# Block-sparse attention and a GELU feed-forward: the first batch as three units of eight query blocks instead of two of twelve

## The chip, the cores and the metric

The kernel runs on one core of a Trainium2 chip. A core has five engines that run in parallel and meet only through semaphores: TensorE (PE in the profile; its weight loads are listed apart as PEld), VectorE (DVE), ScalarE (ACT), GpSimd (POOL) and SyncE (SP, which only issues DMAs here). Each engine takes its instructions in the order in which the program emits them. The metric is the device time of one launch in microseconds; before the change it is 292.93 us, the median of three runs (292.79 to 292.94).

## What is computed

Attention over 4 batches, 8 heads, 768 positions and 64 dimensions, with a block mask of 32 by 32, and behind it a feed-forward layer over the 3072 tokens:

```python
scores = scale * np.matmul(q, k.transpose(0, 1, 3, 2))
mask = np.abs(blk_i - blk_j) <= window          # window = 1
mask = mask | (blk_i == 0) | (blk_j == 0) | (blk_i == n_blocks - 1) | (blk_j == n_blocks - 1)
for qb in range(n_blocks):
    for kb in sampled_blocks[qb]:               # three drawn blocks for each query block
        mask[qb * block:(qb + 1) * block, kb * block:(kb + 1) * block] = True
scores = np.where(mask, scores, -1000000000.0)
...
attn = attn / (np.sum(attn, axis=-1, keepdims=True) + 1e-09)
...
x = np.ascontiguousarray(attn_out.transpose(0, 2, 1, 3)).reshape(B * S, H * D)
h = x @ w_in                                    # 512 x 2048
g = 0.5 * h * (1.0 + erf(h * inv_sqrt2))
return (g @ w_out).astype(np.float32)           # 2048 x 512
```

Query blocks 0 and 23 see all 24 key blocks (they are called dense here). Each of the 22 others sees blocks 0 and 23, itself and its two neighbours, and the three drawn for it; a drawn block that is one of these, or a repeat, is replaced by a spare block whose values are zero.

## The kernel before

**Units.** The work is cut into units (class `Unit`, line 287). A unit is half a batch: twelve query blocks, as three quads of four. Each batch has a first unit with quads 1, 2 and 0 and the two dense blocks (`dense=True`, block 23 too), and a second with quads 3, 4 and 5. So there are eight units. The order of a unit is attention, then FFN1 (x times w_in and Gelu, `ffn1_step`, eight steps of eight matmuls with 384 columns), then FFN2 (g times w_out, 16 matmuls for each quad, `ffn2_pieces`). FFN2 of one unit is not run by itself: its matmuls are the filler of the next unit's attention, a number of them in each round, by a list written by hand (`quota`, and `tail` behind the last round). The first unit has no FFN2 to fill with; it gets products whose result nobody reads (`idle_products`).

**Attention.** `attention` (line 547) runs rounds. A sparse round is two query blocks over all heads: scores (TensorE, line 322, into a score tile of two banks of PSUM, pool `psA`, two buffers, which FFN1's `hp` tiles share), row maxima (VectorE, L347), exponentials (ScalarE, L364), transposition (VectorE, L381). A dense round is one dense block and half the heads (L350, L368, L386). When the rounds of a group are through (a quad, or the two dense blocks), `values` multiplies the probabilities with the values in two halves (TensorE, L442; its result `av` is in pool `psV`, one buffer), `divided` divides by the sums (VectorE, L457 to L461), and `outputs` transposes on TensorE (L471) and copies into `xT`, the input of FFN1 (ScalarE, L479). `when` and the unit's `ends` say in which round each half of each group's product is emitted. The second units of batches 0 to 2 also run the first two dense rounds of the batch after them (`ahead`). Between exponentials and Gelu ScalarE loads another function table (`table`, L392).

**Gathered keys.** The sparse scores read keys from one buffer `gb`, which holds for each query block of the unit at hand its neighbours' keys and the blocks at both ends (`gather_fixed`, lines 265 to 274) and its three drawn blocks, keys and values (`gather`, line 283, one copy for each, at an offset that a register holds). `gb` is refilled for the next unit while FFN1 of the present unit runs: first the fixed part and eight blocks on VectorE, then the rest on GpSimd. `hold_loads` (line 157) is a copy of one element on GpSimd: whatever is behind it on GpSimd, DMA issues too, waits until that element is written. In the very first unit keys and values are gathered apart: the keys first (from `k0`, which lies in the memory of `qT1`), the values by `values_of` in hooks of the rounds, since they land later.

**Loads.** All big loads are issued by GpSimd and share one queue in the order of issue: batch 0's keys, queries and values, w_in in two quarters and a half, w_out in two halves, then for batch 1 the keys (`load_by_token`, line 111) and queries. Keys and queries of batches 1 to 3 are turned by a transposing DMA that SP issues (`turn_keys` line 118, into `ptd`, which later holds dense probabilities; `turn_queries` line 121, into `qT1` for odd batches). SP also issues the stores of the outputs (L502), in the same order as the program. From `ptd` VectorE places the keys, scaled, into `kv` (`place_keys`, line 125; `next_keys` is this and a spare block). For batch 1 that is a hook of the second unit's attention:

```python
attention(nxt, filler, [3, 11, 2, 5, 3, 8, 1, 7, 1], (5,), ahead=units[n + 2],
          hooks={} if n else {
              3: [lambda: next_keys(1)]})
```

The main loop (line 678) goes over the units: refill of `gb` for the next unit and loads within FFN1's first step, FFN1, then the next unit's attention with this unit's FFN2 as its filler.

## Time and profile before

| what | value |
|---|---|
| median of three runs | 292.93 us |
| the profiled execution | 293.46 us, of which its span on the core is 291.7 us |
| mean granted TensorE clock in it | 0.988 |
| PE busy | 262.8 us (90% of the span) |
| DVE busy | 209.4 us (72%) |
| ACT busy | 204.3 us (70%) |
| POOL busy | 118.2 us (41%) |
| DMA | 25.36 MB in 90068 packets, 87 GB/s over the span |
| shares of the chain that ended last | PE 53%, DMA 17%, ACT 15%, POOL 6%, DVE 4%, issue 3% |

A row of the timeline has the start in us from the start of the span, the duration, engine, line and operation, out<-in by the program's names, the shape, how many instructions are merged, and in brackets how long the engine sat idle before them and which instruction ended that. A matmul's duration includes its way through the array; matmuls in a row overlap, so their pace is read from many of them. A row of the chain of waits has start, duration and what. A row of busy time by stretch has for each engine its busy us and number of instructions (PE, PEld, DVE, ACT, POOL), then the granted clock of TensorE as a share of full speed, the busy share of the DMA engines (summed over overlapping transfers) and GB/s. A row of a group has the number of instructions, their busy time in us and the mean duration in ns, then the idle time before them.

### The profile page before, as it was taken

The page shows a single profiled execution, that of the slowest core. Times are in us where ns is not written, and L with a number is a line of the kernel's source. Part 1 is how long each engine was busy: PE and PEld are TensorE (multiplying, and loading weights), DVE is VectorE, ACT ScalarE, POOL GpSimd, SP SyncE. Part 2 cuts the span into 40 slices and gives each one's busy share as a digit, 9 for nine tenths or more (in the row PEclk, how much of TensorE's full clock was granted, in tenths as well). Part 3 has the DMA queues.
Part 4 walks back from the last instruction along what each step waited for, and adds up shares of the span by engine and source line. Part 5 has one row for each costly group of instructions (what it writes and reads, how often), then busy time and mean ns, then how long its engine had stood idle before and what let it go on. Part 6 is the DMA issues. An engine that isn't in the chain of part 4 may idle for free.

```text
span 291.7 us, 11274 instructions
## 1 busy us (share of the span) xinstructions
PE 262.8 (90%) x4803; PEld 142.2 (49%) x4803; DVE 209.4 (72%) x477; ACT 204.3 (70%) x374; POOL 118.2 (41%) x217
## 2 busy tenths in 40 slices
PE   1799899854999999979998999999999999999995
PEld 1624555322553555535553556445544555356644
DVE  7699786816898969588997967798939877781000
ACT  8779656942667975787758966796778766976621
POOL 8789974935696004940594006910040014000000
PEclk9999999995999999999999999999999999999999
DMA  6995599999999215991399118991100110011001
GB/s 105 166 108 98 97 193 190 154 153 199 78 155 171 73 40 121 91 78 44 27 162 175 42 38 146 91 58 38 40 0 31 50 37 1 20 58 39 1 36 73
DMA packets 90068, 25.36 MB, mean 87 GB/s; under 512 B 81697, under 2 KB 86562, under 8 KB 90018
## 3 DMA queue, kind: packets, MB, share of 16 engines
q0 software_dynamic: 67792, 13.64, 87.5%
q1 hardware_dynamic: 22226, 11.01, 16.1%
q8 instruction: 37, 0.61, 1.0%
q14 instruction: 13, 0.11, 0.2%
HBM read 27.26 MB, written 6.29 MB: 115 GB/s over the span
## 4 chain that ended last, share of the span: by engine, by line
PE 53%; DMA 17%; ACT 15%; POOL 6%; DVE 4%; issue 3%; POOLq 1%; ACTq 0%
PE hp L492 19%; PE op L514 16%; PE av L442 9%; DMA ptd<-kn 6%; ACT pp L364 6%; DMA w_out_sb<-in_moe_w_out_dram 5%; ACT L392 4%; DMA kv<-in_v_dram 3%; POOL gb L283 3%; PE sc L322 3%; DMA qn<-in_q_dram 3%; ACT g L495 2%; PE tx L471 2%; PE av L543 2%; PE op L543 2%
## 5 line engine op out<-in xcount | busy, mean ns | idle before, releaser
L364 ACT ACTIVATE pp<-sc,nm 128x256 bf16<-128x256 f32 x176 | 75.3, 544 | 16.2 <-DVE nm L347 15.9
L514 PE MATMUL op<-w_out_sb,g 128*128 128x512 bf16 x336 | 86.4, 381 | 0.2
L492 PE MATMUL hp<-xT,w_in_sb 128*128 128x384 bf16 x512 | 85.0, 326 | 0.8 <-ACT xT L479 0.4
L495 ACT ACTIVATE g<-hp 128x768 bf16<-128x768 f32 (+1 forms) x72 | 52.1, 738 | 31.4 <-PE hp L492 31.4
L492 PEld LDWEIGHTS <-w_in_sb 128*128 128x128 bf16 x512 | 50.0, 98 | 36.0 <-issue 3.1
L347 DVE TENSOR_REDUCE nm<-sc 128x4 f32<-128x1024 f32 (+1 forms) x48 | 52.9, 1108 | 6.9 <-PE sc L322 6.9
L283 POOL COPY gb<-kv 128x388 bf16 (+1 forms) x87 | 36.7, 475 | 26.1 <-DVE gb L274 24.1
L514 PEld LDWEIGHTS <-g 128*128 128x128 bf16 x336 | 28.5, 97 | 35.4 <-issue 11.4
L283 DVE COPY gb<-kv 128x388 bf16 x177 | 39.8, 302 | 0.4 <-DMA qn<-in_q_dram 0.3
L442 PEld LDWEIGHTS <-pT 64*32 64x32 bf16 (+1 forms) x2400 | 26.3, 92 | 23.6 <-DVE pT L381 14.4
L381 DVE STREAM_TRANSPOSE pT<-pp 128x512 f32<-128x512 f32 (+1 forms) x48 | 31.5, 656 | 4.9 <-ACT pp L364 4.6
L442 PE MATMUL av<-kv,pT 64*32 64x130 bf16 (+1 forms) x1344 | 28.2, 223 | 7.4 <-DVE pT L381 7.2
L322 PE MATMUL sc<-gb,qT 64*32 64x256 bf16 x704 | 19.2, 274 | 7.4 <-ACT pp L364 4.7
L479 ACT COPY xT<-tx 128x512 bf16<-128x512 bf16 (+1 forms) x32 | 13.6, 450 | 15.3 <-PE tx L471 15.3
L157 POOL COPY mark<-g 1x1 bf16<-1x1 bf16 x2 | 7.0, 3504 | 42.4 <-ACT g L495 42.4
L133 POOL DMA_DIRECT2D kv<-in_v_dram x32 | 22.6, 715 | 1.3 <-DMA qn<-in_q_dram 1.2
L322 PEld LDWEIGHTS <-qT 64*32 64x32 bf16 x832 | 11.7, 90 | 23.3 <-issue 17.0
L368 ACT ACTIVATE pp<-sc,nm 128x768 bf16<-128x768 f32 x16 | 17.1, 1103 | 6.8 <-DVE nm L350 6.8
L111 POOL DMA_DIRECT2D qn<-in_q_dram x18 | 19.1, 1068 | 6.7 <-DMA w_out_sb<-in_moe_w_out_dram 6.2
L350 DVE TENSOR_REDUCE nm<-sc 128x1 f32<-128x768 f32 x16 | 15.0, 944 | 7.0 <-PE sc L322 6.7
L442 PE MATMUL av<-gb,pT 64*32 64x130 bf16 x1056 | 19.8, 223 | 0.0
L392 ACT ACT_TABLE_LOAD x15 | 19.2, 1283 | 0.3
(73 smaller groups left out, 230.1 us busy)
## 6 DMA issues: line engine op xcount, KB each, us to landing
out_dram<-os SPq DMA_DIRECT2D x23, 256.0 KB, 2.3
kv<-in_v_dram POOLq DMA_DIRECT2D x32, 96.0 KB, 6.9
kn<-in_k_dram POOLq DMA_DIRECT2D x18, 128.0 KB, 5.8
qn<-in_q_dram POOLq DMA_DIRECT2D x18, 128.0 KB, 5.5
w_out_sb<-in_moe_w_out_dram POOLq DMA_DIRECT2D x2, 1024.0 KB, 12.8
w_in_sb<-in_moe_w_in_dram POOLq DMA_DIRECT2D x2, 512.0 KB, 9.9
w_in_sb<-in_moe_w_in_dram POOLq DMA_DIRECT2D x1, 1024.0 KB, 9.0
kn<-in_k_dram POOLq DMA_DIRECT2D x2, 384.0 KB, 5.3
```

The source lines that it names most:

```text
L111: nc.gpsimd.dma_start(out=rows[:, c], in_=src[b, :, P * c:P * c + P].rearrange("h p d -> p h d"))
L133: nc.gpsimd.dma_start(out=kvs[b % 2][32 * hh:32 * hh + 32, 0:NB, c0:c0 + D], in_=v[b, h].rearrange("(n p) d -> p n d", p=BL))
L283: (engine or nc.vector).tensor_copy(sampled(unit.place[j], r)[:, None, c0:c1], src[:, bass.ds(at[j][r], 1), :])
L322: nc.tensor.matmul(o, lhsT=qT[rows, j // 4, pr, BL * (j % 4):BL * (j % 4) + BL], rhs=rhs(rows, pr), start=True, stop=True)
L347: nc.vector.tensor_reduce(out=nm[:, 0:2 * n].rearrange("p (g j) -> p g j", g=2), in_=A4[:, :, 0:n, :], op=ALU.max, axis=AX.X, negate=True)
L364: nc.scalar.activation(at[:, x // n, x % n], A[:, a:a + 256].rearrange("p (e c k) -> p e c k", e=2, k=BL), AF.Exp, bias=nm[:, x:x + 1])
L381: nc.vector.transpose(pt.rearrange("p g c x -> p (g c) x")[:, :, 64 * s:64 * (s + n)].bitcast(F32), pp[:, 0:512 * n].bitcast(F32).rearrang ...
L392: nc.scalar.activation(junk, zero[0:1, 0:1], func)
L442: nc.tensor.matmul(av[32 * s:32 * (s + w), h, V2 * G:V2 * G + V2], lhsT=pv[rows, c % 4, BL * s:BL * (s + w), c // 4], rhs=src[rows], start ...
L492: nc.tensor.matmul(hp[:, i, 0:T], lhsT=w_in_sb[:, ki, (m + i) * P:(m + i + 1) * P], rhs=xTs[n % 2][:, ki, 0:T], start=(ki == 0), stop=(ki ...
L495: nc.scalar.activation(g[:, m + i[0]:m + i[1], 0:T], hp[:, i[0]:i[1], 0:T], AF.Gelu)
L514: nc.tensor.matmul(op, lhsT=g[:, m, t * P:(t + 1) * P], rhs=w_out_sb[:, m, :], start=(m == 0), stop=(m == KOUT - 1))
```

## The change

Batch 0 becomes three units of two quads each: (1, 0) with the dense blocks, (2, 3), and (4, 5). Batches 1 to 3 keep two units of three quads. So there are nine units, and FFN1 of the first three has 256 columns instead of 384. A unit may now begin at a later column of its `xT` (`first`), because the third unit shares a buffer with the first, whose dense rounds already write block 23's columns.

With it go:

- the first unit has eight rounds instead of ten, 27 idle products instead of 43, and other rounds for its products (`when`); the fixed keys of its second sparse group are copied on ScalarE;
- `early` in this unit: the division of the group before the last stands behind the last transposition instead of ahead of the last round's end;
- the product of the unit's last group goes into a score tile (`psA`) instead of the one buffer of `psV`;
- GpSimd's order: no key copies for a third group; `ones(1)` ahead of the first value gather; w_in's second half behind the first value gather; w_out and batch 1's keys behind the second; batch 1's queries only in FFN1 of the first unit, behind a `hold_loads` and the gather of blocks 10 and 11; batch 1's values in FFN1 of the second unit;
- the refill of `gb` for unit 1 is blocks 8, 9 and 12 to 15 on VectorE and 10, 11 on GpSimd, for unit 2 blocks 16 to 19 and 20 to 22 (`SHARES`);
- `next_keys(1)` moves to the second round of the third unit's attention, and the first two dense rounds of batch 1 to the end of that unit;
- new lists of filler for the attentions of units 1, 2 and 3.

```diff
     class Unit:
-        def __init__(self, b, quads, dense):
-            self.b, self.quads, self.dense = b, quads, dense
+        def __init__(self, b, quads, dense, first=0):
+
+            self.b, self.quads, self.dense, self.c0 = b, quads, dense, first
...
-    units = [Unit(b, quads, dense) for b in range(B)
-             for quads, dense in (((1, 2, 0), True), ((3, 4, 5), False))]
+    units = [Unit(0, (1, 0), True), Unit(0, (2, 3), False), Unit(0, (4, 5), False, P)]
+    units += [Unit(b, quads, dense) for b in range(1, B)
+              for quads, dense in (((1, 2, 0), True), ((3, 4, 5), False))]
...
         if half == 0:
-            st[grp, "av"] = psV.tile([P, 2, 512], F32, name="av", tag="V")
+
+            pool, tag = (psA, "A") if grp == units[0].ends[len(units[0].rounds) - 1] else (psV, "V")
+            st[grp, "av"] = pool.tile([P, 2, 512], F32, name="av", tag=tag)
...
-            if weighed and last:
+            if weighed and last and not early:
                 divide()
...
         turned(rounds[n - 1][1])
+        if early:
+            divide()
...
     load_w_in(1)
-    others |= block_numbers(grps[2], POOL)
-    gather(units[0], grps[2], others, 0, KC, nc.gpsimd)
     others |= block_numbers(grps[0], POOL)
+    ones(1)
...
             gather(units[0], grps[t], others, KC, BW, nc.gpsimd)
-            if t == 1:
+            if t == 0:
                 load_w_in(1, 2)
-            if t == 2:
+            else:
                 load_w_out(0, 2)
                 load_w_out(1, 2)
                 load_by_token(kn, k, 1)
-                load_by_token(qn, q, 1)
-                others.update(block_numbers(J1[8:], POOL))
+                others.update(block_numbers(J0[9:], POOL))
...
-    attention(units[0], idle_products(43), [0, 3, 0, 8, 3, 7, 3, 2, 3, 3, 4], (3, 0, 4),
-              when=(5, 6, 7, 7, 8, 9, 10, 11),
-              hooks={0: [lambda: fixed(1)], 1: [lambda: fixed(2, nc.scalar.copy, 0)],
-                     3: [lambda: fixed(2, nc.scalar.copy, 1)], 4: [values_of(0)],
-                     6: [values_of(1)], 8: [values_of(2)], 10: [more_numbers(J1[:6])]})
+    attention(units[0], idle_products(27), [0, 3, 1, 8, 3, 7, 1, 0, 0], (0, 0, 4), early=True,
+              when=(5, 5, 6, 6, 8, 9),
+              hooks={1: [lambda: fixed(1, nc.scalar.copy, 0)], 3: [lambda: fixed(1, nc.scalar.copy, 1)],
+                     4: [values_of(0)], 6: [values_of(1)], 8: [more_numbers(J1[:4])]})
...
+    SHARES = {0: (J0[7:9] + J1[:4], J0[9:]), 1: (J1[4:8], J1[8:])}
...
             if s == 0:
-                if n == 0:
-                    turn_keys()
-                    turn_queries(1)
-                    hold_loads(sampled(nxt.place[J1[7]], NR - 1)[0:1, BW - 1:BW])
-                    gather(nxt, J1[8:], others, engine=nc.gpsimd)
-                    ones(1)
-                    hold_loads(qT1[0:1, 0:1])
-                    load_values(1)
+                if n <= 1:
+                    hold_loads(sampled(nxt.place[mine[-1]], NR - 1)[0:1, BW - 1:BW])
+                    gather(nxt, theirs, others, engine=nc.gpsimd)
+                    if n == 0:
+                        load_by_token(qn, q, 1)
+                        turn_keys()
+                        turn_queries(1)
+                        others.update(block_numbers(J1[8:], POOL))
+                    else:
+                        hold_loads(qT1[0:1, 0:1])
+                        load_values(1)
...
+        elif n == 0:
+            attention(nxt, filler, [3, 5, 5, 6, 5], (1, 0, 5), hooks={0: [more_numbers(J1[4:8])]})
+        elif n == 1:
+            attention(nxt, filler, [3, 7, 2, 5, 2, 5, 1], (4,), ahead=units[3],
+                      hooks={0: [more_numbers(J0[:3])], 1: [lambda: next_keys(1)]})
+        elif n == 2:
+            attention(nxt, filler, [1, 5, 3, 2, 1, 3, 3, 5, 3], (1, 0, 4))
         elif fresh:
             attention(nxt, filler, [1, 7, 4, 3, 1, 5, 4, 7, 6], (2, 0, 6))
         elif b + 1 < B:
-            attention(nxt, filler, [3, 11, 2, 5, 3, 8, 1, 7, 1], (5,), ahead=units[n + 2],
-                      hooks={} if n else {
-                          3: [lambda: next_keys(1)]})
+            attention(nxt, filler, [3, 11, 2, 5, 3, 8, 1, 7, 1], (5,), ahead=units[n + 2])
```

18 lines of the change are left out of this document (8 added, 10 removed).

## The prediction, made before the changed kernel was run

> **What bounds the kernel now.** I read the page's slices first (TensorE is busy in nine tenths of the span), then the timeline of the first 112 us, then the chain of waits, then busy time and clock by stretches. FFN1 (hp, line 492) marks the units: it starts when a unit's attention is over.
>
> ```profile
> 39.39 10.56 PE L492 MATMUL hp<-xT,w_in_sb 128*128 128x384 bf16 x64 [0.41 <-ACT xT L479]
> ...
> 78.49 3.71 PE L492 MATMUL hp<-xT,w_in_sb 128*128 128x384 bf16 x20
> ...
> 111.19 10.56 PE L492 MATMUL hp<-xT,w_in_sb 128*128 128x384 bf16 x64
> ...
> 60.53 2.12 PE L514 MATMUL op<-w_out_sb,g 128*128 128x512 bf16 x8
> ...
> 66.43 1.17 DVE L125 TENSOR_SCALAR kv<-ptd 128x768 bf16<-128x768 bf16 x4 [6.21 <-DMA ptd<-kn]
> ...
> 69.53 0.85 PE L442 MATMUL av<-kv,pT 64*128 64x130 bf16 x28 [6.88 <-DVE pT L381]
> ```
>
> The first FFN1 starts at 39.39; all before is attention with nothing else for TensorE to do. The next starts 39.10 us later, the third 32.70 later. The first interval holds a hole: TensorE ends its eight products at 62.65 and starts the next matmul at 69.53, 6.88 idle. VectorE, in order, stands for 6.21 us at line 125, where batch 1's keys are placed, because their transposing DMA has not landed. The chain of waits shows why it is late:
>
> ```profile
> 35.46 15.09 DMA w_out_sb<-in_moe_w_out_dram
> ...
> 56.24 10.17 DMA ptd<-kn
> ```
>
> The second half of w_out lands at 50.55, the keys, asked for behind it, at 56.24, and the transposition takes 10.17 more, to 66.41. The hole has a second price, in the granted clock (the column after POOL's):
>
> ```profile
> 64.00:66.00 2.00, 0.00 (x0) 0.00 (x0) 0.00 (x0) 0.00 (x0) 0.00 (x0) 1.00 1.22 123
> ...
> 66.00:68.00 2.00, 0.00 (x0) 0.00 (x0) 1.50 (x7) 0.00 (x0) 0.00 (x0) 0.56 1.24 281
> ...
> 72.00:74.00 2.00, 2.00 (x66) 1.08 (x64) 0.86 (x4) 1.60 (x2) 2.00 (x3) 0.73 2.66 124
> ```
>
> From 66 to 74 the clock is between half and three quarters (first and last of four rows). So the 39.10 us hold more than the 6.88 in waste, and the 39.39 before them is what a shorter first unit can cut. From 111.19 on both kernels run the same list of work on batches 1 to 3, so I follow the changed kernel to that point, the start of FFN1 of batch 1's first unit, and compare: before, two FFN phases stand ahead of it, after, three.
>
> **The start, until the first FFN1.**
>
> ```profile
> 16.21 0.98 DVE L265 COPY gb<-qT 128x768 bf16<-128x768 bf16 x3
> ...
> 17.61 0.36 DVE L274 COPY gb<-qT 128x768 bf16<-128x768 bf16 x1
> ...
> 22.44 8.36 POOL L283 COPY gb<-kv 128x260 bf16 x24 [1.58 <-PE sc L322]
> ...
> 22.50 3.29 ACT L364 ACTIVATE pp<-sc,nm 128x256 bf16<-128x256 f32 x8
> ...
> 30.74 0.74 POOL L146 DMA_DIRECT2D w_in_sb<-in_moe_w_in_dram  x1
> ...
> 31.48 3.16 POOL L283 COPY gb<-kv 128x260 bf16 x9
> ...
> 37.46 0.16 DVE L457 TENSOR_SCALAR den<-av 96x8 f32<-96x8 f32 x1 [1.78 <-PE av L442]
> ...
> 38.50 1.80 DVE L684 COPY kv<-qT 128x3200 bf16<-128x3200 bf16 x1
> ```
>
> ```profile
> 12.40 9.71 DMA kv<-in_v_dram
> ```
>
> Unit 0 has 8 rounds instead of 10: two sparse rounds go, at 3.29/2 = 1.65 us of ScalarE each. The fixed copies of its second group leave VectorE, where they lay from 16.21 to 17.97, for ScalarE, in the place of the third group's, and the sparse exponentials come about 0.5 earlier, at 22.0. Twelve of GpSimd's key copies go; `ones(1)` moves into its idle time ahead of 22.44 and costs nothing while the value load, landing at 12.40 + 9.71 = 22.11, ends that wait; without that cover it costs its eight memsets, once. Then GpSimd copies 12 value blocks (half of 8.36), issues w_in (0.74) and copies 9 more (3.16): 22.44 + 4.18 + 0.74 + 3.16 = 30.5. The last group's value products need those nine and end near 31.3; without that new wait they would end some 0.7 sooner. It takes most of what the score tile and the later division (`early`) bring: the last group's products no longer wait for the division of the group before (one lasts from 37.46 to 38.50, 1.04; I take 0.3 of it, bounds 0 and 1.04). In the old kernel the last division starts at 37.46 and FFN1 at 39.39, 1.9 later: 31.3 + 1.9 = **33.2** (32.6 to 34.2), 6.2 earlier.
>
> **Unit 1 (blocks 8 to 15).**
>
> ```profile
> 34.59 1.76 POOL L151 DMA_DIRECT2D w_out_sb<-in_moe_w_out_dram  x2
> ...
> 36.33 5.28 POOL L111 DMA_DIRECT2D kn<-in_k_dram  x6
> ...
> 43.76 4.17 DVE L283 COPY gb<-kv 128x388 bf16 x24
> ...
> 55.80 4.13 POOL L283 COPY gb<-kv 128x388 bf16 x9
> ...
> 49.99 0.87 ACT L495 ACTIVATE g<-hp 128x384 bf16<-128x384 f32 x2 [0.49 <-PE hp L492]
> ...
> 50.88 1.28 ACT L392 ACT_TABLE_LOAD   x1
> ...
> 52.28 3.20 ACT L364 ACTIVATE pp<-sc,nm 128x256 bf16<-128x256 f32 x8
> ```
>
> ```profile
> 286.75 1.76 PE op L543 x16
> ```
>
> ```profile
> L347 DVE TENSOR_REDUCE nm<-sc 128x4 f32<-128x1024 f32 (+1 forms) x48 | 52.9, 1108 | 6.9 <-PE sc L322 6.9
> ...
> L381 DVE STREAM_TRANSPOSE pT<-pp 128x512 f32<-128x512 f32 (+1 forms) x48 | 31.5, 656 | 4.9 <-ACT pp L364 4.6
> ```
>
> ```profile
> 26.00:28.00 2.00, 1.99 (x94) 1.11 (x88) 1.90 (x4) 1.74 (x5) 2.00 (x7) 1.00 0.01 2
> ```
>
> No unit has 256 columns in FFN1 yet; the nearest row is the last product, 16 matmuls of 256 columns in 1.76, 0.110 each. The other bound is the 384-column row, 10.56/64 = 0.165. I take 0.110, since three phases then cost what two cost before (3 x 64 x 0.110 = 21.1 = 2 x 10.56): FFN1 is 7.0, ending at 40.2. VectorE's refill no longer hides with room: from 32.4 the key copy (1.80), the fixed copies (3.46 before, from 40.30 to 43.76, for twelve blocks; 2.6 for eight) and 18 gathers at 4.17/24 = 0.174 (3.1) end at 40.0. `hold_loads` keeps GpSimd back until then; behind it wait its copies of blocks 10 and 11, six at 4.13/9 = 0.46, until 42.8. These are the second round's, no longer the last round's: TensorE, in order, stands at those scores with FFN2's products queued behind them from about 41.6 to 42.9. The exponentials restart 2.3 after FFN1 (52.28 against 49.99) at 42.5 and would take the second round at 44.1; its maxima are ready near 44.5, so 0.4 of the 1.2 reaches ScalarE. All loads move up with GpSimd: w_in's second half from 30.74 to 26.6, w_out from 34.59 to 30.5, the keys from 36.33 to 32.3; DMA keeps its order and is free then (share 0.01 from 26 to 28), so w_out is whole at 50.55 - 4.1 = 46.4. FFN2 wants its ninth slice at about 45.2: another 1.2 on TensorE, some 0.5 of it on the chain. Each further round costs VectorE 1.11 + 0.66: the fourth maxima end at 44.5 + 2 x 1.77 + 0.5 = 48.5, its exponentials (1.65) at 50.2. The first group's products lie behind 11 filler products and its division ahead of the last transposition on VectorE, so that this ends near 52.9 (my reckoning of the orders; 51 if nothing is in its way). Products of the last group, about 1.4, and the 1.9 of unit 0 bring FFN1 to **56.2**, 23.0 after the last; 21.5 at the tight end, 25 at the loose one.
>
> Each more unit costs two changes of function table. Here the table starts at 50.88 and the first exponential at 52.28: 1.40. [...]
>
> **Unit 2 (blocks 16 to 22, and two dense rounds of batch 1).**
>
> ```profile
> 62.93 4.35 SPq L121 DMA_TRANSPOSE qT<-qn  x1
> ...
> 68.87 0.18 POOL L157 COPY mark<-qT 1x1 bf16<-1x1 bf16 x1 [7.70 <-DMA qT<-qn]
> ...
> 120.64 2.84 DVE L125 TENSOR_SCALAR kv<-ptd 128x768 bf16<-128x768 bf16 x4 [3.55 <-DMA ptd<-kn]
> ```
>
> FFN1 runs to 63.2, exponentials restart at 65.5. The keys of batch 1 land at 52.1 and their transposition at 62.3; VectorE asks after the second exponentials, at about 69. The 6.21 is gone with 7 us in hand. The queries' load now stands behind GpSimd's held copies, and their transposition on SP behind the keys', as in the row at 62.93: it lands at about 65, and only the dense scores near 73 want it. But placing the keys now stands between two rounds of a short unit: 1.17 in the row at 66.43, 2.84 at 120.64 beside GpSimd's load issues, which are due here too (values of batch 1, 65 to 71). I take 2.0, and TensorE waits for it once, since only 5 filler products are left to it. GpSimd's nine copies (4.13) end by 64 and are wanted at 67. Stores queue on SP behind the transpositions until 63; two of three buffers are in use then, so nobody waits. Next FFN1 at **79.5** (23.3; 21.5 to 25.5).
>
> **Unit 3 (batch 1).**
>
> ```profile
> 77.98 2.01 DVE L265 COPY gb<-kv 128x1536 bf16<-128x1536 bf16 x3
> ...
> 81.70 7.74 DVE L283 COPY gb<-kv 128x388 bf16 x27 [0.28 <-DMA qn<-in_q_dram]
> ...
> 89.84 1.98 DVE L350 TENSOR_REDUCE nm<-sc 128x1 f32<-128x768 f32 x2 [0.41 <-PE sc L322]
> ...
> 91.69 2.05 ACT L368 ACTIVATE pp<-sc,nm 128x768 bf16<-128x768 f32 x2
> ...
> 93.31 1.22 DVE L347 TENSOR_REDUCE nm<-sc 128x4 f32<-128x1024 f32 x1
> ...
> 106.06 0.17 DVE L457 TENSOR_SCALAR den<-av 128x8 f32<-128x8 f32 x1 [0.60 <-PE av L442]
> ```
>
> Here the change pays back. VectorE's refill for 11 blocks is unchanged and took from 77.98 to 89.44, 11.46 us, with 27 copies at 7.74/27 = 0.287 beside GpSimd's load issues. It fitted under an FFN1 of 10.56; FFN1 now takes 8 (7.0, and 1.0 of waiting for the first Gelu behind the table). The dense maxima wait for VectorE until 79.3 + 11.46 = 90.7 and take 0.99; from the first dense exponential to the first sparse maxima it is 93.31 - 91.69 = 1.62, so these come at 93.3, as before. From there 17.88 us remained in the old kernel. VectorE had few waits in them, 0.60 at 106.06 the largest before the end, so 14 fewer filler products of FFN2 free little: I take 17.2, bounds 16.4 and 18.0. FFN1 of unit 3 at **110.5**, against 111.19.
>
> The sum: 33.2 + 23.0 + 23.3 + 31.0 = 110.5, 0.7 less than before. The profiled execution took 293.46 (its span 291.70, 1.76 around it) and would take 292.8; the median of the runs shown is 292.93, 0.53 below the profiled one, so the forecast is 292.2. The terms' bounds, not all at one end at once, give it 290.2 to 294.4.
>
> **The rivals.**
>
> *Unit 3 starves TensorE (slower).* After its first two dense scores and 6 filler products TensorE has nothing until the exponential: from about 89.9 to 92.8 in my account, 2.9 us. In the row from 64 to 66 the clock is still full, from 66 on, 3.35 after the last product, it is half. If VectorE's refill ends a microsecond later, the gap grows past that point and decides: 1.0 for the delay and, over the next 6 us at half clock, some 3 more: 110.5 + 4.0 = 114.5, time 296.2. For it: the refill shares its time with load issues. Against: the attention that follows has slack on TensorE. [...]
>
> *The loads are not earlier (slower).* If w_out's flow keeps its old end, 50.55, unit 1's FFN2 stands 4 us longer, of which 3 reach the end: 295.2. Against: the share of 0.01 when w_in is now asked for.
>
> *The short units run tight (faster).* The waits of units 1 and 2 (0.4, 0.5, 2.0 and the late restarts) vanish behind their fillers: 21.7 each instead of 23.0 and 23.3, and the last stretch 16.6: 3.5 less, 288.7. For it: steady intervals show only about a microsecond without work; against: four rounds hide less than six.
>
> **How the numbers follow.** The forecast case has 0.56, the starved unit 0.16, the late loads 0.07, the tight units 0.17; 0.04 is left for worse. A measurement of this kernel can tell about 0.2%, 0.6 us, from no change: below 292.3 is faster, above 293.5 slower. The forecast case, 290.2 to 294.4 about 292.2, splits 0.28 faster, 0.14 same, 0.14 slower; with the rivals that is 0.45, 0.14 and 0.41. The range that holds the time 8 in 10 reaches to both neighbours: 288.4 to 296.4.
>
> **What would show it.** Right: FFN1 starts near 33.2, 56.2, 79.5 and 110.5; no wait of VectorE at line 125; a wait of TensorE for GpSimd's gather in unit 1's second scores; VectorE's gather ending after FFN1 in unit 3; the granted clock at 1.00 from 20 us on. Wrong: an FFN1 of 256 columns much above 7 us, a gap over 3 us on TensorE with a lower clock behind it, w_out landing after 47, or unit 3's attention visibly shorter than 17 us from its first sparse maxima.

## The result, and the profile after

The changed kernel takes 302.42 us (median of four runs, 301.1 to 303.51), the kernel before 292.94 beside it (292.79 to 292.99): a ratio of 1.0322, with a 95% interval from 1.0277 to 1.0368. The prediction, 292.2 in 288.4 to 296.4, is wrong: 10 us too low, and on the wrong side. On some of the chips used below the kernel before itself was disturbed in most executions and took 297 to 302; ratios are made from the undisturbed ones, so runs on different chips are compared by their ratios.

The timeline of the changed kernel on TensorE (start, length, engine, line, tiles, count, and in brackets the idle time ahead with what ended it). FFN1 is now at line 496, value products at 446, FFN2 at 518.

```profile
36.09 7.88 PE L496 MATMUL hp<-xT,w_in_sb 128*128 128x256 bf16 x64 [0.41 <-ACT xT L483]
...
62.20 7.20 PE L496 MATMUL hp<-xT,w_in_sb 128*128 128x256 bf16 x64
...
88.33 7.42 PE L496 MATMUL hp<-xT,w_in_sb 128*128 128x256 bf16 x64
...
120.27 10.56 PE L496 MATMUL hp<-xT,w_in_sb 128*128 128x384 bf16 x64 [0.19 <-ACT xT L483]
...
29.49 0.89 PE L446 MATMUL av<-gb,pT 64*32 64x130 bf16 x15
32.91 0.23 PE L446 MATMUL av<-gb,pT 64*32 64x130 bf16 x3 [2.53 <-issue]
...
59.40 0.35 PE L446 MATMUL av<-kv,pT 64*32 64x130 bf16 x21 [2.18 <-issue]
...
84.31 0.30 PE L446 MATMUL av<-kv,pT 64*32 64x130 bf16 x12 [1.99 <-issue]
...
51.83 0.81 PE L518 MATMUL op<-w_out_sb,g 128*128 128x512 bf16 x3 [1.33 <-ACT os L504]
...
77.28 0.38 PE L518 MATMUL op<-w_out_sb,g 128*128 128x512 bf16 x1 [1.23 <-ACT os L504]
...
110.09 0.59 PE L518 MATMUL op<-w_out_sb,g 128*128 128x512 bf16 x2 [2.29 <-ACT os L504]
```

The FFN1 starts were forecast at 33.2, 56.2, 79.5 and 110.5. Nearly all of the loss lies ahead of the fourth, 9.08 of the 9.5 us between the two spans: it starts that much behind the old 111.19, and from there to the end the kernels take 180.5 (before) and 180.9. Two kinds of waiting are new. In each of the first three units TensorE stops for 2.0 to 2.5 us in the middle of a group's value products, put down to "issue", which means that nothing the profile shows was missing. And in units 1 to 3 FFN2's 17th product waits for the copy of the first quad's output (`os`, line 504), 1.33 + 1.23 + 2.29 = 4.85 in all.

By stretches of 2 us (busy time of PE, PEld, DVE, ACT and POOL, then the granted clock, the DMA share and GB/s) the clock falls behind the first and third stop, and not behind the second, which ends at 59.40:

```profile
34.00:36.00 2.00, 1.64 (x7) 0.75 (x7) 1.97 (x3) 0.87 (x3) 2.00 (x3) 0.55 1.09 157
36.00:38.00 2.00, 1.91 (x11) 1.45 (x11) 1.97 (x4) 0.37 (x3) 1.41 (x2) 0.60 1.19 193
...
60.00:62.00 2.00, 1.95 (x14) 0.97 (x16) 1.77 (x5) 0.81 (x2) 0.00 (x0) 1.00 1.57 150
...
86.00:88.00 2.00, 2.00 (x10) 0.88 (x9) 2.00 (x5) 0.69 (x3) 1.66 (x3) 0.50 0.00 0
```

So FFN1 takes 7.88 in unit 0 and 7.42 in unit 2, and 7.20 in unit 1, where the clock stays at 1.00. VectorE's rows show that the hole of the old kernel is gone as forecast, no wait at line 125, and that unit 3's maxima come late:

```profile
74.96 1.37 DVE L125 TENSOR_SCALAR kv<-ptd 128x768 bf16<-128x768 bf16 x4
...
97.88 1.81 DVE L352 TENSOR_REDUCE nm<-sc 128x1 f32<-128x768 f32 x2
...
100.51 1.22 DVE L349 TENSOR_REDUCE nm<-sc 128x4 f32<-128x1024 f32 x1
```

The clue to the stops is in the page's list of DMA queues (packets, MB, share):

```profile
q8 instruction: 38, 0.62, 0.9%
```

0.62 MB in 38 packets is 16 KB each. TensorE's program has 4851 weight loads, as many products and some 32 semaphore and drain instructions, 9734 in all: 256.2 to a packet. Experiment 3 adds 2048 instructions to the kernel before, and its page lists 45 packets instead of 37, eight more, 256 instructions for each; its timeline has a stop at every 128 products, which with their weight loads are 256 instructions. So in these runs one packet brings a block of 256 TensorE instructions. I counted TensorE's instructions in the trace, in their order, up to the first one behind each stop:

```
run               first instr.  remainder  block entered  packet starts  goes on   stop
                  behind stop   by 256     at us          at us          at us     us
after                 962         194        27.47          30.54         32.91    2.76
after                1730         194        53.08          56.92         59.40    2.41
after                2499         195        78.24          81.92         84.31    2.21
lists16               962         194        27.86          32.14         34.60    4.12
lists16              1730         194        53.13          57.13         59.65    2.31
shift128             1219         195        30.74          34.40         36.77    2.72
shift192             1218         194        31.27          34.98         37.37    3.99
shift192             1986         194        57.77          61.64         64.11    2.71
split96_lists16      1730         194        48.26          52.20         55.17    2.06
before_split96       1475         195        33.87          37.42         39.79    2.82
small_stream        10434         194       295.90         296.96        299.63    2.62
small_stream        11202         194       306.81         307.91        310.26    1.91
```

(The rows below "after" are experiments, told further down; a stop runs from the start of the last weight load ahead of it to that of the first behind it.) The remainder is 194 or 195 at every stop, so the stops stand whole blocks apart, where a block ends. That it is not 0 would fit some 62 instructions ahead of the first one that the trace lists, which is not shown. In these rows the packet for the next block starts after TensorE has entered the current one, 3.07, 3.84 and 3.68 us later in the changed kernel, and there TensorE goes on 2.4 us after the packet has started. Where the current block was used up sooner, TensorE stood still: from 53.08 to 56.99 the block was used up in 3.91 us; the next could run after 6.32.

**Theory:** TensorE runs dry at block ends, because value products use up 256 instructions in less time than the next block takes to come, and because loads in flight put off its packet. The new loads' order puts them under the value products, and a unit of two quads is some 768 instructions long, three blocks, so that the ends (962, 1730, 2499) meet the same place in each unit. The waits for the output copy are a second, smaller cause. **Rivals:** a wait for data, a bank or a semaphore at a fixed place in the value products; the score tile and the later division; or the output copies alone.

### The profile page after: what moved, and what is told of

It is laid out like the page before. It is cut to its first block, busy times and chain, and to the rows that moved or that the text cites. A ratio compares the mean times of both kernels' runs of the same rounds, so it can differ in the third digit from the quotient of the medians.

```text
span 301.2 us, 11299 instructions
## 1 busy us (share of the span) xinstructions
PE 255.7 (85%) x4796; PEld 147.3 (49%) x4851; DVE 209.8 (70%) x483; ACT 209.3 (69%) x388; POOL 110.9 (37%) x200
## 4 chain that ended last, share of the span: by engine, by line
PE 56%; ACT 17%; DVE 10%; issue 7%; DMA 6%; POOL 3%; POOLq 0%; DVEq 0%; ACTq 0%
PE hp L496 24%; PE op L518 13%; PE av L446 11%; ACT pp L366 8%; ACT L394 4%; DMA kv<-in_v_dram 3%; DVE nm L349 3%; DMA qn<-in_q_dram 3%; ACT g L499 2%; PE sc L324 2%; PE tx L475 2%; DVE gb L283 2%; POOL gb L283 2%; PE av L547 2%; PE op L547 2%
## 5 line engine op out<-in xcount | busy, mean ns | idle before, releaser
L496 PE MATMUL hp<-xT,w_in_sb 128*128 128x384 bf16 (+1 forms) x576 | 86.2, 310 | 0.9 <-ACT xT L483 0.6
L518 PE MATMUL op<-w_out_sb,g 128*128 128x512 bf16 x285 | 77.1, 385 | 9.8 <-ACT os L504 4.9
L499 ACT ACTIVATE g<-hp 128x768 bf16<-128x768 f32 (+3 forms) x81 | 53.6, 675 | 31.2 <-PE hp L496 31.2
L496 PEld LDWEIGHTS <-w_in_sb 128*128 128x128 bf16 x576 | 56.9, 99 | 31.1 <-issue 3.6
L283 POOL COPY gb<-kv 128x388 bf16 (+1 forms) x81 | 35.3, 490 | 27.1 <-DVE gb L274 24.4
L283 DVE COPY gb<-kv 128x388 bf16 x183 | 41.2, 304 | 0.1
L483 ACT COPY xT<-tx 128x192 bf16<-128x192 bf16 (+2 forms) x33 | 13.7, 444 | 25.8 <-PE tx L475 25.6
L133 POOL DMA_DIRECT2D kv<-in_v_dram x32 | 25.6, 807 | 1.6 <-DMA qn<-in_q_dram 1.1
L461 DVE TENSOR_SCALAR den<-av 128x8 f32<-128x8 f32 (+2 forms) x28 | 4.5, 162 | 27.4 <-PE av L446 26.9
L370 ACT ACTIVATE pp<-sc,nm 128x768 bf16<-128x768 f32 x16 | 17.2, 1104 | 7.6 <-DVE nm L352 7.5
L157 POOL COPY mark<-g 1x1 bf16<-1x1 bf16 x2 | 3.8, 1914 | 43.8 <-ACT g L499 43.8
```

Of the source, the lines that this page charges most:

```text
L133: nc.gpsimd.dma_start(out=kvs[b % 2][32 * hh:32 * hh + 32, 0:NB, c0:c0 + D], in_=v[b, h].rearrange("(n p) d -> p n d", p=BL))
L283: (engine or nc.vector).tensor_copy(sampled(unit.place[j], r)[:, None, c0:c1], src[:, bass.ds(at[j][r], 1), :])
L370: nc.scalar.activation(pp[:, 0:S].rearrange("p (c k e) -> p c e k", e=2, k=BL), A[:, 0:S].rearrange("p (c e k) -> p c e k", e=2, k=BL), AF ...
L496: nc.tensor.matmul(hp[:, i, 0:T], lhsT=w_in_sb[:, ki, (m + i) * P:(m + i + 1) * P], rhs=xTs[n % 2][:, ki, c0:c0 + T], start=(ki == 0), sto ...
L499: nc.scalar.activation(g[:, m + i[0]:m + i[1], 0:T], hp[:, i[0]:i[1], 0:T], AF.Gelu)
L518: nc.tensor.matmul(op, lhsT=g[:, m, t * P:(t + 1) * P], rhs=w_out_sb[:, m, :], start=(m == 0), stop=(m == KOUT - 1))
```

## The experiments

**1. Moving the block ends.** 64 or 96 small products go ahead of the first transposition, so that 128 or 192 more instructions precede the same work. They were meant to fit into the wait for the keys.

```diff
+    op = psO.tile([P, D_MODEL], F32, name="op")
+    for _ in range(64):                  # 96 in shift192
+        nc.tensor.matmul(op[0:64, 0:64], lhsT=identity[0:64, 0:64], rhs=identity[0:64, 0:64],
+                         start=True, stop=True)
     for (which, pr), bank in zip([(w, pr) for w in "kq" for pr in range(NPR)], spaces()):
```

> 64 small products (64x64x64, 128 TensorE instructions) stand ahead of the first transposition, where TensorE waits for the keys until 6.30 us. Theory (instruction blocks): TensorE's program comes in blocks of 256 instructions, and the three stops stand where a block ends; 128 instructions more move every block end by half a block. In the profile of after a fetch starts 0.3 to 1.1 us after TensorE enters a block where no load runs and up to 3.9 us after it where loads run, and the next block can run 2.4 us after the fetch starts. By these, the stops of 2.76, 2.41 and 2.21 us leave their places (32.9, 59.4 and 84.3 us), what is left of stops before unit 3 adds up to about 3 us instead of 7.4, and the time falls by 3 to 6 us, to 296.5 to 299.5. Rival (a fixed place: a wait for data, a bank or a semaphore in the value products): the three stops stay at the same products with the same length, and the time stays within 1 us of 302.4.

> 96 small products (192 instructions) ahead of the first transposition. Theory (instruction blocks): the block ends come into the second half of the first value products and the middle of the last, blocks of 256 instructions are then used up in 2.7 to 3.6 us, and the stops before unit 3 add up to about 9 us, more than in after: 303 to 306 us, the stops at other products than in after. Rival (a fixed place): the stops stay where they are, within 1 us of 302.4. Rival (more early work helps in itself, whatever its phase): the same gain as with 128 instructions.

Measured: 299.73 (ratio 1.0231, 1.0183 to 1.0278) with 128, and 308.07 (1.055, 1.049 to 1.0609) with 192; the changed kernel itself is at 1.0322. On TensorE's timeline, first with 128:

```profile
3.91 3.62 PE L641 MATMUL op<-identity 64*64 64x64 bf16 x64 [3.91 <-POOL identity masks.py:199]
...
36.77 0.33 PE L475 MATMUL tx<-identity,xh 96*128 96x96 bf16 x4 [2.83 <-issue]
```

then with 192:

```profile
3.91 5.33 PE L641 MATMUL op<-identity 64*64 64x64 bf16 x96 [3.91 <-POOL identity masks.py:199]
...
37.37 0.52 PE L446 MATMUL av<-gb,pT 64*32 64x130 bf16 x17 [3.72 <-issue]
...
64.11 0.30 PE L446 MATMUL av<-gb,pT 64*32 64x130 bf16 x13 [2.48 <-issue]
```

The stops went to other products, to the transposition of outputs even, and in the table they stand at a block's end again. Nothing that waits at a fixed place would do this, and more early work does not help in itself.

The times say less than the places do. The added products could start only when `identity` was written, at 3.91, and did not fit into the wait: the first transposition starts at 7.46 and 9.17 instead of 6.30. With 192 the first value products are 3.49 late (30.71 against 27.22) ahead of both stops in the table, and a block's end at 15.12 explains 1.01 of that at most. The two stops add up to 6.70 where about 9 was expected. So its 308.07, 2 us beyond the expected end, is in large part the late start and does not measure the block ends. With 128 the time falls in spite of a start delayed by 2.35 (29.57), to 0.2 above the expected 299.5. About half of that gain lies behind unit 3's FFN1, most of it in one unit (32.70 instead of 33.61), and why is open but for a stop of 0.55 at 181.29 that is gone.

**2. Without the traffic.** The values of batch 1 are not loaded (`load_values(1)` is left out in unit 1's FFN1).

> The values of batch 1 are not loaded (left out; batch 1 is computed with the zeros that stand there). Theory (the fetch stands behind the loads in flight): the block that TensorE enters at 78.2 us is then fetched within 1.1 us instead of 3.7, and the stop of 2.21 us at 84.3 falls below 0.5 us; the stops at 32.9 and 59.4 stay. Rival (the fetch is late because TensorE's sequencer is too busy with value products, loads or not): the third stop stays at 2 us or more.

Measured in a single run, TensorE's timeline in place of the third stop:

```profile
82.98 0.55 PE L446 MATMUL av<-kv,pT 64*32 64x130 bf16 x24
83.32 0.38 PE L446 MATMUL av<-gb,pT 64*32 64x130 bf16 x18
83.49 0.45 PE L446 MATMUL av<-kv,pT 64*32 64x130 bf16 x28
```

No stop: the last group runs through. The DMA queues say why. In the changed kernel, from the block's entry at 78.2 until 81.9, there is no instruction packet, and the values fill the queues (a share above 100% means that packets overlap):

```profile
q0 software_dynamic: 1599, 0.20, 315.5%
q1 hardware_dynamic: 141, 0.26, 26.0%
```

and from 81.9 to 84.3, with the last packet of the values (q0) through at 81.24, it comes, at 81.92:

```profile
q8 instruction: 1, 0.02, 2.8%
```

Without the values the block was entered at 79.75 and its packet started at 80.80, 1.05 later instead of 3.68, and unit 2 took 22.69 (63.73 to 86.42) instead of 26.13. The first two stops stayed (3.98 and 2.21), as expected. The whole run, 307.02, was longer than the changed kernel's, and not because of this edit's place: unit 3's FFN1 starts at 120.62 there and 120.27 in the changed kernel, most of the other 4 us come later, some at block ends (1.29 at 170.6). It is a single run, and where the rest went stays open.

**3. The price by itself.** 1024 products like the value products stand behind the last output of the kernel before, where no load runs.

```diff
+        small = psA.tile([P, 2, 512], F32, name="hp", tag="A")
+        for i in range(1024):
+            h, s = i % 2, i // 2 % 4
+            rows = slice(64 * h, 64 * h + 64)
+            nc.tensor.matmul(small[32 * s:32 * s + 32, h, 0:128], lhsT=identity[rows, 0:32],
+                             rhs=identity[rows, :], start=True, stop=True)
```

> The kernel before with 1024 products of the value products' kind (64x32 weights, 128 columns, 2048 TensorE instructions) behind the last output's products, where no load runs; they feed nothing. Theory (instruction blocks): a block of 256 takes these products 1.85 us at their pace in the profile of before (52 in 0.75 us), but its successor can run only 0.3 to 1.1 + 2.4 us after TensorE entered it, so each block takes 2.7 to 3.5 us, with a stop of 0.9 to 1.6 us at each block's end (seven or eight of them, 256 instructions apart), 22 to 28 us in all. Rival (blocks are there in time unless loads run): 1024 x 0.0144 = 14.8 us without a stop above 0.3 us.

Measured in a single run (318.41), the end of TensorE's timeline:

```profile
289.15 1.39 PE L550 MATMUL hp<-identity 64*32 64x128 bf16 x143
292.17 1.27 PE L550 MATMUL hp<-identity 64*32 64x128 bf16 x128 [1.63 <-issue]
295.90 1.52 PE L550 MATMUL hp<-identity 64*32 64x128 bf16 x128 [2.46 <-issue]
...
303.08 1.91 PE L550 MATMUL hp<-identity 64*32 64x128 bf16 x128 [1.54 <-issue]
...
313.72 1.78 PE L550 MATMUL hp<-identity 64*32 64x128 bf16 x113 [1.55 <-issue]
```

The trace cuts the stream into groups of 128 products, 256 instructions, with a stop ahead of each. From 292.17 to 313.72 six blocks pass, 3.59 us each; the packets start 1.06 to 1.16 us after the entry of a block, and the next block runs 2.3 to 2.7 us after that. So with no load at all TensorE gets 256 instructions in some 3.6 us, a little above the 2.7 to 3.5 expected. The products themselves take 1.27 at first and 1.91 at the end, where the granted clock is 0.50 (300 to 302), and the stop is shorter by about as much: it is the blocks that set the pace.

**4. The filler lists.** In units 1 to 3 one partial sum of the list becomes 16, as in the kernel before, so that the output copy is asked for before the 17th product.

```diff
-            attention(nxt, filler, [3, 5, 5, 6, 5], (1, 0, 5), hooks={0: [more_numbers(J1[4:8])]})
+            attention(nxt, filler, [3, 5, 5, 3, 8], (1, 0, 5), hooks={0: [more_numbers(J1[4:8])]})
...
-            attention(nxt, filler, [3, 7, 2, 5, 2, 5, 1], (4,), ahead=units[3],
+            attention(nxt, filler, [3, 7, 2, 4, 3, 5, 1], (4,), ahead=units[3],
...
-            attention(nxt, filler, [1, 5, 3, 2, 1, 3, 3, 5, 3], (1, 0, 4))
+            attention(nxt, filler, [1, 5, 3, 2, 1, 4, 2, 5, 3], (1, 0, 4))
```

> The filler lists of units 1 to 3 are cut so that one of their sums is 16, so the output copy is asked for before the second quad's first product stands in TensorE's order; nothing else moves. Theory: the waits for the copy at the 17th product (1.33, 1.23 and 2.29 us) go, which in units 1 and 2 is partly taken back at the next wait for exponentials or at the stop; the three stops stay (7.4 us). The time falls by 1 to 3.5 us, to 299 to 301.5. Rival (these waits only fill time in which TensorE would wait for exponentials anyway): within 0.6 us of 302.4.

Measured: 299.0 (1.0208, 1.017 to 1.0246), 1.1% or 3.3 us better than the change. The waits for line 504 are gone from TensorE's timeline, but not all of the gain is theirs: unit 2's block is fetched 1.9 us after its entry at 79.47 and its stop is gone too, while the stop of unit 0 is 4.12 in this execution (FFN1 at 38.84). How long that stop is differs between executions: its packet started 4.28 us after the block's entry here, 3.07 in the changed kernel.

**5. The score tile undone alone.**

```diff
-            pool, tag = (psA, "A") if grp == units[0].ends[len(units[0].rounds) - 1] else (psV, "V")
-            st[grp, "av"] = pool.tile([P, 2, 512], F32, name="av", tag=tag)
+            st[grp, "av"] = psV.tile([P, 2, 512], F32, name="av", tag="V")
...
-    attention(units[0], idle_products(27), [0, 3, 1, 8, 3, 7, 1, 0, 0], (0, 0, 4), early=True,
+    attention(units[0], idle_products(27), [0, 3, 1, 8, 3, 7, 1, 0, 0], (0, 0, 4),
```

> That part of the change alone is undone: the last group of the first unit writes its value products to the value tile again, and its division stands at its old place. Theory (instruction blocks and output copies): this part is nearly free here, because its gain ends in the first stop; the products wait for the bank until the division of the group before has read it (30.2 us against a start at 28.94), some 1.3 us, and the block's end, 2 to 4 us behind, comes later by as much or less, so the fetch has more time: 0.5 us faster to 1 us slower than 302.4. Rival (the score tile holds up the next scores or the division behind the last transposition costs): 2 us or more faster.

Measured: 304.88 (1.0426, 1.0232 to 1.062). The interval holds the change's own ratio, so the size stays open; the rival, 2 us faster, is ruled out but for the interval's lower end. All three stops are there (3.31, 2.02, 2.21).

**6. Both causes together.** The lists of experiment 4, and a shift by 96 that takes no time ahead of the keys:

```diff
+        for i in range(m):
+            w = 128 if i < 16 else 512
+            for c in range(0, 512, w):
+                nc.tensor.matmul(op[:, c:c + w], lhsT=identity, rhs=rhs[:, c:c + w],
+                                 start=True, stop=True)
```

> Two things together: the filler lists cut at 16, and the block ends moved by 96 instructions at no place ahead of the keys: 16 of the 27 idle products of the first unit are done as four of 128 columns each. Theory (instruction blocks): no block of the value products before unit 3 is then used up faster than its successor can come, but for one in unit 2 or 3 (1 to 2 us); of the 4.1 and 2.3 us of stops in the run with the lists alone 4 to 6 go, and the time comes to 293.5 to 296.5. That would be the change's own effect without its stops: still not faster than before. Rival (the stops are only one face of a chain that is as long by itself): within 1.5 us of the 299.0 of the lists alone.

Measured: 295.49 (1.007, 1.0037 to 1.0103). TensorE's timeline:

```profile
34.27 1.48 PE L496 MATMUL hp<-xT,w_in_sb 128*128 128x256 bf16 x12 [0.41 <-ACT xT L483]
...
55.17 0.34 PE L446 MATMUL av<-kv,pT 64*32 64x130 bf16 x17 [1.84 <-issue]
...
60.05 7.20 PE L496 MATMUL hp<-xT,w_in_sb 128*128 128x256 bf16 x64
...
83.14 1.91 PE L496 MATMUL hp<-xT,w_in_sb 128*128 128x256 bf16 x16
...
114.47 10.56 PE L496 MATMUL hp<-xT,w_in_sb 128*128 128x384 bf16 x64 [0.19 <-ACT xT L483]
```

Of the change's 3.2%, 1.1 went with the lists and 1.4 more with the block ends; 0.7% is left. (The profiled execution is one of 297.16, and unlike experiment 1 this shift leaves the first transposition where it was.) The stop left in unit 1 (2.06) stands behind a block entered at 48.26, whose packet came at 52.20. GpSimd had asked for the last of the queries at 51.74, but their packets went on until about 56.5, so a packet can come while a load runs.

**7. The queries later**, first behind the first Gelu of unit 1, then behind the first output of its first group:

```diff
+                    if n == 1:
+                        hold_loads(g[0:1, 0, 0:1])       # late_queries2: xTs[1][0:1, 0, 0:1]
+                        load_by_token(qn, q, 1)
+                        turn_queries(1)
...
                     if n == 0:
-                        load_by_token(qn, q, 1)
                         turn_keys()
-                        turn_queries(1)
```

> As the run with 96 instructions and the lists cut at 16, and the queries of batch 1 are asked for when unit 1's FFN1 has begun (near 61 us) instead of at 44.7 us, so that no load of theirs runs while TensorE enters the block at 48.3 us. Theory (a fetch waits behind the loads in flight): that fetch starts within 1.5 us of the entry instead of 3.94, and the stop of 2.06 us at 55.2 us falls below 0.7; the queries, transposed near 72 us, still come in time for batch 1's first scores at 73, or hold them up by 1 us at most. The time is 293 to 295.5 on a chip where the kernel before takes 292.7: 0 to 1% slower than before. Rival (the transposition of the keys, not the queries' load, keeps the fetch waiting): the stop stays near 2 us. Rival (the queries come too late): a new wait for them at the first scores of batch 1, above 2 us, and no gain.

> As late_queries, and the queries of batch 1 are asked for as soon as the first output of unit 1's first group is in place (near 54 us instead of 58). Theory: the block entered at 48.3 us is still fetched in time, the queries are transposed some 3 us earlier, the wait of 2.88 us for them at batch 1's first scores falls below 1, and unit 3's FFN1 starts at 111 to 114 us instead of 116.45; the ratio to the kernel before comes to 0.998 to 1.008. Rival (another cause keeps it behind): no stop or wait above 1 us is left on TensorE before unit 3, and unit 3's FFN1 still starts after 115 us.

Measured: 297.99 (1.0132, 1.0068 to 1.0196), and 297.59 (0.9961, 0.9922 to 1.0). The last ratio rests on two times of the kernel before, 292.76 and 296.1, and I do not take it for a gain: the best of the twelve runs is 295.71. TensorE in late_queries:

```profile
34.55 7.15 PE L496 MATMUL hp<-xT,w_in_sb 128*128 128x256 bf16 x64 [0.41 <-ACT xT L483]
...
56.75 7.20 PE L496 MATMUL hp<-xT,w_in_sb 128*128 128x256 bf16 x64
...
75.27 0.83 PE L324 MATMUL sc<-kv,qT 64*32 64x512 bf16 x8 [2.88 <-DMA qT<-qn]
```

Unit 1's stop is gone (packet 1.93 after the entry at 48.34, a little over the 1.5 expected), and the queries are late instead: the second rival came true along with the theory. In late_queries2, GpSimd asks for the queries at 58.13 instead of 59.07, not near 54 as meant, because the first output is copied only at 57.67. TensorE's wait for them is then 1.08, but VectorE's refill for unit 3 starts late (in the profiled execution, which at 300.15 is the slowest of the twelve):

```profile
88.53 7.00 DVE L283 COPY gb<-kv 128x388 bf16 x27 [3.60 <-DMA qn<-in_q_dram]
```

With that, unit 3's FFN1 starts at 116.01, not at 111 to 114. The values, asked for behind the queries, are the likely late part; the row names only what landed last.

**8. The kernel before with its own hole and its own block ends.** Four edits: the keys placed one round later (`4: [lambda: next_keys(1)]` for `3:`); the block ends moved by 96 as in experiment 6; and the keys of batch 1 loaded between the two halves of w_out, with unit 1's list `[3, 5, 0, 8, 6, 9, 1, 8, 2]`, once with the values held for the queries and once without.

> The kernel before, with one edit: VectorE is asked for the keys of batch 1 (66.43 us, behind a wait of 6.21) one round later in unit 1. Theory (VectorE stands in order): one transposition and one round of maxima, and with them a half group of value products on TensorE, go ahead of the wait; TensorE's hole of 6.88 us falls to about 5, and the time falls by 1 to 3 us, to 289.7 to 291.7. Rival (the keys' landing sets the end of this unit whatever stands ahead): within 0.6 us of 292.7.

> The kernel before, and only the block ends moved by 96 instructions, with 16 of the 43 idle products done as four of 128 columns each. Theory (instruction blocks): the kernel before pays 0.5 to 0.6 us at a block's end where it pays at all; moved by 96, two ends come behind blocks of value products that are used up in 3.1 to 3.2 us while loads run, near 37 and 76 us, with stops of about 2.4 us each: 294.7 to 297. Rival (the fetch matters only in units of two quads): within 0.6 us of 292.7.

> The kernel before, with the load order and one filler list changed: the keys of batch 1 are asked for between the two halves of w_out instead of behind them, and unit 1's filler is laid so that the second half of w_out is wanted later. Theory (the keys' landing, 56.24 and, transposed, 66.41 us, sets the end of unit 1, as putting the wait one round later has shown): the keys land about 6 us earlier, VectorE's wait of 6.21 us falls below 2, and the time falls by 2 to 5 us, until the queries, which still come last, hold the first scores of batch 1. Rival (another transfer takes the place at once: queries, values or w_out's second half): within 1 us of the kernel before.

> As the last, and the values of batch 1 are asked for without waiting for the queries' transposition. Theory: if the values' landing is what unit 2's copies wait for next, this gives 0.5 to 2 us more than the run before; if their small packets get in the way of the transpositions or of TensorE's instruction blocks, it takes 0.5 to 3 us away. No effect within 0.5 us would say that neither counts.

Measured: 0.9994 (0.995 to 1.0039), 1.0043 (1.0005 to 1.0081), 1.018 (1.0046 to 1.0314) and 1.0387 (1.0268 to 1.0506). Three of the four expected sizes were missed; the second, 1.007 to 1.015 as a ratio, is missed by the middle of the interval and reached by its end. TensorE with the keys one round later:

```profile
70.08 0.51 PE L322 MATMUL sc<-kv,qT 64*32 64x512 bf16 x8 [3.45 <-DMA qT<-qn]
...
78.58 10.87 PE L492 MATMUL hp<-xT,w_in_sb 128*128 128x384 bf16 x64
```

The hole moves to the queries and unit 2's FFN1 stays where it was (78.49). With the block ends moved by 96:

```profile
39.79 0.24 PE L442 MATMUL av<-kv,pT 64*32 64x130 bf16 x4 [2.60 <-issue]
...
42.45 11.30 PE L492 MATMUL hp<-xT,w_in_sb 128*128 128x384 bf16 x64 [0.41 <-ACT xT L479]
...
69.05 0.86 PE L442 MATMUL av<-kv,pT 64*128 64x130 bf16 x28 [3.51 <-DVE pT L381]
...
79.00 10.86 PE L492 MATMUL hp<-xT,w_in_sb 128*128 128x384 bf16 x64
```

One of the two expected stops came, and 3 us of delay in unit 0 became 0.5 at unit 2: the hole gave it up, 3.51 instead of 6.88. The kernel before has the same weakness, and a hole that hides it. The execution of experiment 3, whose program is the kernel before until its end, shows it with nothing moved:

```profile
38.61 0.34 PE L442 MATMUL av<-kv,pT 64*32 64x130 bf16 x14 [2.22 <-issue]
...
41.59 10.56 PE L492 MATMUL hp<-xT,w_in_sb 128*128 128x384 bf16 x64 [0.41 <-ACT xT L479]
```

Its first FFN1 is 2.2 late, and its second, at 78.97, only 0.5. With the keys ahead of w_out's second half, batch 1's first scores wait for the queries (2.79 us; 10.33 with the values let loose).

**9. All loads of the kernel before earlier.**

```diff
+    load_w_in(1, 2)
...
-            if t == 1:
-                load_w_in(1, 2)
-            if t == 2:
+            if t == 0:
                 load_w_out(0, 2)
                 load_w_out(1, 2)
+            if t == 1:
                 load_by_token(kn, k, 1)
+            if t == 2:
                 load_by_token(qn, q, 1)
```

> The kernel before, with GpSimd asking for all loads one step earlier: w_in's second half at the end of the start, w_out behind the first value copies, keys and queries behind the second and third. Theory (DMA stood idle from 26 to 31 us, so every load behind it comes some 5 us earlier): VectorE's wait of 6.21 us for the keys falls below 2.5, the queries follow in time, and the time falls by 1 to 4 us: a ratio of 0.986 to 0.997. Against it works what the instruction blocks say: the value products of unit 0, from 30 to 36 us, now run under loads, so one stop of 2 to 3 us comes there and delays unit 0, which the hole takes up. Rival (the order of landing, not the time of asking, sets the hole, or the new stop eats the gain): within 0.3% of the kernel before.

Measured: 297.66 on a chip where the kernel before had a median of 299.18 (292.76 to 302.25), with no ratio to be had: unclear. Its profiled execution (296.35, span 294.6) on TensorE:

```profile
30.00 0.40 PE L322 MATMUL sc<-gb,qT 64*32 64x256 bf16 x13 [1.89 <-issue]
...
36.19 1.34 PE L524 MATMUL op<-qT,identity 128*128 128x512 bf16 x3 [3.41 <-issue]
...
45.38 10.56 PE L492 MATMUL hp<-xT,w_in_sb 128*128 128x384 bf16 x64 [0.41 <-ACT xT L479]
...
77.08 10.86 PE L492 MATMUL hp<-xT,w_in_sb 128*128 128x384 bf16 x64
...
109.78 10.56 PE L492 MATMUL hp<-xT,w_in_sb 128*128 128x384 bf16 x64
```

and on VectorE, with batch 3's keys:

```profile
185.93 1.21 DVE L125 TENSOR_SCALAR kv<-ptd 128x768 bf16<-128x768 bf16 x4 [4.52 <-DMA ptd<-kn]
```

The hole is gone without a third unit: unit 1 takes 31.70 instead of 39.10. But two stops of 2.17 and 3.48 us come in unit 0, which starts its FFN1 6 us later. The second stands at the same instruction as the old kernel's wait of 0.55 at 31.30, now with loads running. At unit 2's FFN1 this execution is still 1.41 ahead of the kernel before (109.78 against 111.19). It falls behind later: between the FFN1 of units 4 and 5 it takes 34.40 instead of 29.92, with VectorE waiting 4.52 instead of 1.68 for batch 3's keys. So the block ends take part of what the loads gain, and this later stretch takes the rest and more. That VectorE's wait is what lengthens it is read from one trace, and why those keys are late was not tested. No version tried is shown to beat the kernel before.

## Why the prediction was wrong

**The step that failed** is the term of each unit's value products. The prediction puts them at their pace ("need those nine and end near 31.3", "Products of the last group, about 1.4") and costs the loads' move ("All loads move up with GpSimd") by when each lands and who wants it. Neither has a price for TensorE's own program, which comes as DMA packets too (q8 in the page's list, 38 in this kernel). It was in sight: the old timeline had idle time put down to issue at a block's end, 0.55 at 31.30, and the idle DMA behind it, quoted from 26 to 28 as free room for loads, went with a short stop (the packet came 0.99 us after the block's entry at 27.96); with all loads earlier, in experiment 9, the same instruction waits 3.41, its packet coming 3.73 after the entry at 30.00. The FFN1 starts lie 2.89, 3.11, 2.83 and 0.94 above the four terms, 9.77 in all. Into the first three go stops of 2.76, 2.41 and 2.21, and the clock behind two of them: against unit 1's 7.20, FFN1 is 0.68 longer in unit 0 and 0.22 in unit 2.

**The second miss** is the first quad's output copy. The filler lists were read as counts of work, and that the old ones reach exactly 16 was not noticed. In units 1, 2 and 3 it is a new wait of 1.33, 1.23 and 2.29, worth with what it moved 1.1% of the time.

**Right** were the other sizes. Freed of stops and with the lists of experiment 4, each unit comes near its term, though no one run has all four: unit 0 to 34.27 (forecast 33.2; experiment 6), unit 1 in 22.20 (56.75 - 34.55; forecast 23.0), unit 2 in 23.09 (83.14 - 60.05; forecast 23.3), unit 3 in 31.33 (114.47 - 83.14; forecast 31.0). Their sum is 110.9 against 110.5. That this is what the change would do without its stops is pieced together, not run. FFN1 of 256 columns takes 7.15 to 7.20 at full clock (7.0), the wait at line 125 is gone, the keys and queries are in time, VectorE's refill in unit 3 ends after FFN1, at 97.88. Two waits on unit 1's chain, 0.4 and 0.5 in the sum, did not come: TensorE waits 0.33 instead of 1.2 for GpSimd's gather, and not at all for the ninth slice of w_out.

**Unit 3** was 0.9 above its term and has the error in another place: the first sparse maxima come at 100.51, 12.2 after FFN1 instead of 13.8, and then it takes 19.76 to the next, with the 2.29 for the copy, instead of 17.2.

**The rivals.** None of them is what happened. The nearest is the starved unit with its fall of the clock; a fall there was, but in units 0 and 2, behind a stop that no data caused, and of 2.53 and 1.99 us rather than over 3; that the forecast's gap of 2.9 in unit 3 would cost no clock was an estimate from the one fall in the trace of before, 3.35 after the last product, and these two came behind shorter stops. The loads were earlier, as the forecast had it, and that was part of the harm, as experiment 9 shows for unit 0. The chance of 0.04 for "worse" was too small: the sum had no case for a wait that the trace of before shows only in small.

## What to carry to other kernels

Count a change in TensorE's instructions too: where 256 of them in a row took less than some 3.6 us with no load (experiment 3), or less than the 5.4 to 6.9 from a block's entry to the next instruction in the table's stops under loads, TensorE could stand at the block's end; idle time put down to "issue" inside a run of small products, with an instruction packet ahead of its end, is the sign. Loads that fit into free DMA time may still be in the way of the program (experiment 2: the packet started 1.05 us after the block's entry without the values and 3.68 with them), so a place under large products (FFN1) looks better than one under small ones; the runs that moved a load there (experiment 7) lost the gain to late landings (waits of 2.88 and 1.08 us for the queries). And a filler list that crossed the end of an output's accumulation waited for the copy of that output (1.33, 1.23 and 2.29 us); with the copy asked for ahead of the 17th product these waits were gone (experiment 4).

## What the runs showed of the hardware that was not expected

With no data moving, in the added stream of experiment 3, a block's packet starts 1.06 to 1.16 us after TensorE enters the block ahead of it; in the table's stops under loads it starts 3.1 to 4.3 us after it. From its start to the next instruction it is 2.3 to 3.0 us in both. This holds for the stops and not for every block: elsewhere a packet can start ahead of the entry (266.46 against 266.56 in the changed kernel). The stops differ between executions: the first is 2.76 us in one, 4.12 and 3.98 in others with the same code up to there. And the length of a stop alone does not decide about the clock: it fell behind stops of 2.53 us (0.55 from 34 to 36) and 1.99 (0.50 from 86 to 88), and stayed behind one of 2.18 (1.00 from 60 to 62).
